# Attention with decay, a gated product and a SwiGLU layer on one core: a second set of Q and K tiles, movable copies, and a scheduler with other durations

## The chip, the core and the metric

The kernel runs on one core of a Trainium2 chip. Five engines work side by side: TensorE (PE; the loading of its weights is listed as PEld), VectorE (DVE), ScalarE (ACT), GpSimd (POOL), and SyncE (SP), which issues the DMAs. They wait for each other through semaphores. The metric is device time in microseconds (us), the median of several runs.

## The reference

Three computations, with independent inputs, all in float32. Cut to what matters:

```python
# attention: q, k, v [4, 8, 576, 64], f [4, 8, 576]
scores = matmul(q, k.T) / sqrt(64)
cum = cumsum(log(clip(f, 1e-4, 1)), axis=-1)
scores = where(causal, -1e9, scores + cum[..., :, None] - cum[..., None, :])
attn = exp(scores - max(scores)); attn /= sum(attn) + 1e-9
x = matmul(attn, v)                    # 4 batches x 8 heads
# product of two projections: x [2304, 512], d_ff 1024
y = ((x @ w1) * (x @ w2)) @ w3 @ w_out
# second layer: x [2304, 512], d_ff 1536
xn = x / sqrt(mean(x * x) + 1e-6) * rms_g
g = xn @ w_gate
out = (g / (1 + exp(-g)) * (xn @ w_val)) @ w_out
```

The kernel chains them: the attention's result (as 2304 tokens of 512) is the x of the product, and its y is the x of the second layer.

## The kernel before

**Numbers.** Each float32 operand of a matmul is held as two tiles, a high part and a low part (value minus high part). A product takes three matmuls (high by high, low by high, high by low). Making the two parts is work for ACT, DVE and POOL: `sub` (L230) is the subtraction that makes a low part and may go to DVE or POOL, `scaled` (L238) a copy with a factor.

**Weights.** They arrive in units of 1 MB in four raw buffers (`nrm`, `ul`, `x`, `x1`). `unit` (L481 to L505) recovers each unit's values in place, 1024 columns at a time: an ACT Prelu (L496), a DVE TENSOR_SCALAR (L497) and a DVE SCALAR_TENSOR_TENSOR (L498). Then ACT copies the high part (L504), and a `sub` (L230) makes the low part, in one piece of 1024 columns or four of 256. The matrix w3 @ w_out is formed first (`wc_group`, L557 to L561, high part `Wch` on ACT, low part `Wcl` on DVE), so that the product layer is one matmul less deep.

**Heads.** For each of 32 heads: `prep` (L345 to L356) makes the high and low parts of Q/8 and K. Q's first low part is a DVE instruction with three operands (L352). The tiles Q1, Q2, K1 and K2 exist once, so a head's parts can be written only when the matmuls of the head before have read them. The two rows that carry the cumulated decay are loaded by a DMA for each (L355, L356), from a copy in DRAM that the start writes. The raw q and k have two buffers. `attn_s` then does the scores: matmuls (L367, L368) into PSUM, the row maxima with the mask on DVE (`row_max`, L384, a custom instruction), the exponentials with row sums on ACT (`row_exp`, L391). Transposes follow (PE L428, high part `PTh` on ACT L431, low part `PTl` on DVE L432), the product with V (PE L451 and L457, ACT copies one half, L461, DVE adds, L462), and for each pair of heads the normalization (PE L473, DVE L477).

**Layers.** `x_split` (L578, L579) makes the parts of the attention's result, `ab_group` (L590 to L600) the two projections and their product `u` (ACT L596, DVE L598) with its parts `uh` (ACT L599) and `ul` (DVE L600), `y_group` (L613) the product with Wc, `norm` (L628) the rms norm, `gv` (L714) and `wout` (L745) the second layer.

**The start** (L782 to L818) clips f, takes the logarithm (ACT L791), the running sum (DVE scan L792), its high part (a DVE cast, L794), its low part, and the rows of head 0; then it writes all rows to DRAM.

**What sets the order.** Every instruction is an entry of a list scheduler, `Plan` (L70 to L192). An entry has one or several engines it may go to, each with a planned duration (`t_dve`, `t_act`, `t_pool`, L210 to L217), what it reads and writes, and perhaps a due time. `begins` turns due times into latest starts from the end backwards; `order` goes through the program in planned time, gives each engine the entry with the smallest due time plus WAIT times the time by which it would start later than the first possible one, and adds MARGIN or MARGIN2 to the lag of results that come after the planned time MT. Constants (L41 to L51) give due times of heads, groups and units. The result is a fixed order for each engine.

Of the kernel before, what the change touches and what calls it, by code (L numbers as in the profile page):

```python
# [22 lines left out]
P = 128  # L23
# [7 lines left out]
CH = S // 2  # L31
# [3 lines left out]
NRAW = 4  # L35
# [34 lines left out]
class Plan:  # L70
# [54 lines left out]
    def order(self):  # L125
# [10 lines left out]
        dma = 0  # L136
# [59 lines left out]
def body(ctx, tc, q, k, v, f, w12, w3, wo1, wgv, wo2, g, out):  # L196
# [35 lines left out]
    def scaled(n, o, a, by, r=(), w=()):  # L232

        def run(e):
            if e == "ACT":
                A.activation(o, a, AF.Copy, scale=by)
            else:
                on[e].tensor_scalar(out=o, in0=a, scalar1=by, scalar2=1.0, op0=ALU.mult, op1=ALU.mult)  # L238

        plan.op([t_act(n), t_dve(n, 0.52, True), t_pool(n, 0.83)], run, r, w)  # L240
# [49 lines left out]
    Wch = [m1.tile([P, DM], F32R, name=f"Wch{i}") for i in range(KF)]  # L290
    Wcl = [m1.tile([P, DM], F32R, name=f"Wcl{i}") for i in range(KF)]
# [38 lines left out]
    def make_qk_rows():  # L330
        for t in (Q2, K2):
            V.memset(f32(t)[D:P, :], 0.0)
# [12 lines left out]
    def prep(h, at):  # L345
        p = h % 2
        a, b_ = rq[p][0:D], rk[p]
        act(S, lambda: A.activation(Q1[0:D, :], a, AF.Copy, scale=0.125), [("rq", p)], ["Q1h"], at)
        act(S, lambda: A.copy(K1, b_), [("rk", p, 0), ("rk", p, 1)], ["K1"], at)
        scaled(S, Q2[0:D, :], a, 0.125, [("rq", p)], ["Q2"])  # L350
        low = dict(out=Q1[D:P, :], in0=a, scalar=0.125, in1=f32(Q1[0:D, :]), op0=ALU.mult, op1=ALU.subtract)
        dve(S + 100, lambda: V.scalar_tensor_tensor(**low), [("rq", p), "Q1h"], ["Q1l"], at, lock=True)  # L352
        sub(S, K2[0:D, :], b_[0:D], f32(K1[0:D, :]), [("rk", p, 0), "K1"], ["K2"])
        if h:
            dma(9200, lambda: SP.dma_start(out=f32(Q2[D:D + 4, :]), in_=cq_d[h]), ["cdq"], ["rowq"], at)  # L355
            dma(9200, lambda: SP.dma_start(out=f32(K2[D:D + 4, :]), in_=cn_d[h]), ["cdn"], ["rown"], at)  # L356
# [20 lines left out]
    def row_max(h, ap, i, key, at):  # L377
# [558 lines left out]
```

## Time and profile before

| | us |
|---|---|
| median of 3 runs | 1038.04 |
| the runs | 1037.55, 1038.04, 1038.85 |
| profiled execution | 1038.35 |
| its span in the trace | 1036.6 |
| around the span | 1.75 |
| PE busy in the span | 992.6 |
| DVE, ACT, POOL busy | 555.5, 466.1, 186.8 |

PE is busy for 96% of the span, and for 91% of it the chain of work that ended last runs through PE. DVE makes up 6%. The mean granted clock of TensorE is 0.99 of full speed. The difference of span and PE's busy time lies almost all in the first sixth of the span, where the attention of the first batch and the unpacking of the weights run side by side. The rest of the heads (three batches) is spread between the matmuls of the layers later on.

### The profile page before, as it was taken

The page shows a single profiled execution, that of the slowest core. Times are in us where ns is not written, and L with a number is a line of the kernel's source. Part 1 is how long each engine was busy: PE and PEld are TensorE (multiplying, and loading weights), DVE is VectorE, ACT ScalarE, POOL GpSimd, SP SyncE. Part 2 cuts the span into 40 slices and gives each one's busy share as a digit, 9 for nine tenths or more (in the row PEclk, how much of TensorE's full clock was granted, in tenths as well). Part 3 has the DMA queues.
Part 4 walks back from the last instruction along what each step waited for, and adds up shares of the span by engine and source line. Part 5 has one row for each costly group of instructions (what it writes and reads, how often), then busy time and mean ns, then how long its engine had stood idle before and what let it go on. Part 6 is the DMA issues. An engine that isn't in the chain of part 4 may idle for free.

```text
span 1036.6 us, 15402 instructions
## 1 busy us (share of the span) xinstructions
PE 992.6 (96%) x5928; PEld 886.8 (86%) x5928; DVE 555.5 (54%) x1104; ACT 466.1 (45%) x1004; POOL 186.8 (18%) x222
## 2 busy tenths in 40 slices
PE   1799979999999999999999999999999999999997
PEld 1578869999999999999999888878888888888896
DVE  6889999757668676776557445532122112211121
ACT  4778887656665665665445434421121112111111
POOL 3535433322523132240220300000000000000000
PEclk9999989999999999999999999999999999999999
DMA  8554533111212121200432324312001000100000
GB/s 271 184 189 134 181 116 120 49 36 51 71 37 61 48 60 39 59 15 1 170 120 105 136 109 162 104 59 84 1 1 41 1 1 0 41 1 1 17 25 21
DMA packets 28161, 75.71 MB, mean 73 GB/s; under 512 B 3644, under 2 KB 12348, under 8 KB 23160
## 3 DMA queue, kind: packets, MB, share of 16 engines
q1 hardware_dynamic: 28088, 74.73, 22.1%
q8 instruction: 46, 0.75, 0.3%
q14 instruction: 27, 0.22, 0.1%
HBM read 64.69 MB, written 10.03 MB: 72 GB/s over the span
## 4 chain that ended last, share of the span: by engine, by line
PE 91%; DVE 6%; DMA 1%; ACT 1%; issue 1%; POOL 0%; ACTq 0%; DVEq 0%; POOLq 0%
PE bank L714 29%; PE bank L590 19%; PE bank L613 10%; PE wide L745 8%; PE bank L745 6%; PE bank L428 5%; PE wide L451 4%; PE bank L557 3%; PE bank L368 1%; PE bank L367 1%; PE wide L473 1%; PE wide L367 1%; PE wide L368 1%; PE wide L457 1%; DMA rk<-in_k 1%
## 5 line engine op out<-in xcount | busy, mean ns | idle before, releaser
L721 DVE TENSOR_TENSOR s<-bank,s 128x512 f32<-128x512 f32 (+1 forms) x60 | 38.3, 638 | 281.3 <-PE bank L714 281.3
L714 PE MATMUL bank<-xnh,wgh 128*128 128x512 f32 (+1 forms) x480 | 177.6, 370 | 0.0
L714 PE MATMUL bank<-xnl,wgh 128*128 128x512 f32 (+1 forms) x480 | 177.6, 370 | 0.0
L714 PE MATMUL bank<-xnh,wgl 128*128 128x512 f32 (+1 forms) x480 | 177.2, 369 | 0.0
L720 ACT ACTIVATE s<-bank 128x512 f32<-128x512 f32 (+1 forms) x60 | 33.3, 555 | 189.4 <-PE bank L714 189.2
L714 PEld LDWEIGHTS bank<-xnh,wgh 128*128 128x128 f32 x480 | 90.2, 188 | 16.9
L714 PEld LDWEIGHTS bank<-xnl,wgh 128*128 128x128 f32 x480 | 90.3, 188 | 16.4
L714 PEld LDWEIGHTS bank<-xnh,wgl 128*128 128x128 f32 x480 | 90.2, 188 | 16.1
L431 ACT CAST PTh<-bank 128x320 fp32r<-128x320 f32 (+3 forms) x128 | 64.7, 506 | 86.5 <-PE bank L428 74.4
L722 ACT CAST zh<-s 128x512 fp32r<-128x512 f32 (+1 forms) x60 | 34.7, 578 | 129.7 <-DVE s L721 129.7
L432 DVE TENSOR_TENSOR PTl<-bank,PTh 128x320 fp32r<-128x320 f32 (+3 forms) x128 | 74.7, 588 | 22.2 <-ACT PTh L431 21.4
L613 PE MATMUL bank<-uh,Wch 128*128 128x288 f32 x256 | 77.2, 302 | 0.0
L613 PE MATMUL bank<-ul,Wch 128*128 128x288 f32 x256 | 75.5, 295 | 0.0
L613 PE MATMUL bank<-uh,Wcl 128*128 128x288 f32 x256 | 75.3, 294 | 0.0
L723 DVE TENSOR_TENSOR zl<-s,zh 128x512 fp32r<-128x512 f32 (+1 forms) x60 | 39.1, 652 | 30.4 <-ACT zh L722 30.0
L451 PE MATMUL wide<-PTh,V 128*128 128x512 f32 (+4 forms) x160 | 53.2, 338 | 0.6 <-DVE nmaxb L384 0.5
L451 PE MATMUL wide<-PTl,V 128*128 128x512 f32 (+4 forms) x160 | 49.6, 326 | 1.9 <-DVE PTl L432 1.9
L596 ACT COPY a<-bank 128x288 f32<-128x288 f32 x64 | 25.6, 400 | 52.7 <-PE bank L590 52.4
L745 PE MATMUL wide<-wo2h,zh 128*128 128x512 f32 x120 | 47.9, 399 | 0.7 <-ACT o L755 0.7
L613 PEld LDWEIGHTS bank<-uh,Wch 128*128 128x128 f32 x256 | 48.1, 188 | 0.4
L613 PEld LDWEIGHTS bank<-ul,Wch 128*128 128x128 f32 x256 | 48.2, 188 | 0.3
L598 DVE TENSOR_TENSOR u<-bank,a 128x288 f32<-128x288 f32 x64 | 29.1, 455 | 35.5 <-PE bank L590 30.5
(281 smaller groups left out, 2589.2 us busy)
## 6 DMA issues: line engine op xcount, KB each, us to landing
raw<-in_wgv SPq DMA_DIRECT2D x12, 1024.0 KB
rk<-in_k SPq DMA_DIRECT2D x64, 144.0 KB
raw<-in_wo SPq DMA_DIRECT2D x6, 1024.0 KB
nrm<-in_w SPq DMA_DIRECT2D x5, 1024.0 KB
rv<-in_v SPq DMA_DIRECT2D x32, 160.0 KB
rq<-in_q SPq DMA_DIRECT2D x32, 144.0 KB
yn_d<-nrm SPq DMA_DIRECT2D x8, 576.0 KB
raw<-yn_d SPq DMA_DIRECT2D x4, 1024.0 KB
```

What stands on the lines that cost most here:

```text
L428: T.transpose(o[:, c * P:(c + 1) * P], PB[p][i][:, kb * P:(kb + 1) * P], ident)
L431: act(n, lambda: A.copy(PTh[:, pt:pt + n], o[:, lo:lo + n]), [], [("PTh", pt), key], at, 55)
L432: dve(n, lambda: V.tensor_sub(PTl[:, pt:pt + n], o[:, lo:lo + n], f32(PTh[:, pt:pt + n])), [("PTh", pt)], [("PTl", pt), key], at)
L451: pe(w, lambda s_=s_, o=o, w=w, c=c, kb=kb, m=m, src=src: T.matmul(t[:, o:o + w], V2[p][:, kb, :], src[:, c:c + w], start=(s_ == 0 and m = ...
L590: T.matmul(o, a, x[:, kt, :], start=(kt == 0 and i == 0), stop=(kt == KD - 1 and i == 2))
L613: T.matmul(o, a[:, es], x[:, ft, :], start=(ft == 0 and i == 0), stop=(ft == KF - 1 and i == 2))
L714: T.matmul(t[m], a[:, m, kt, :], x[:, kt, 0:n], start=(kt == 0 and i == 0), stop=(kt == KD - 1 and i == 2))
L720: act(n, lambda: A.activation(s_()[:, 0:n], t[0], AF.Silu), [("bank", b_[0]), "right"], ["s"], at)
L721: dve(n, lambda: V.tensor_mul(s_()[:, 0:n], t[1], s_()[:, 0:n]), [("bank", b_[1])], ["s"], at)
L722: act(n, lambda: A.copy(zh()[:, 0:n], s_()[:, 0:n]), ["s"], [("zh", zp)], at)
L723: dve(n, lambda: V.tensor_sub(zl()[:, 0:n], s_()[:, 0:n], f32(zh()[:, 0:n])), ["s", ("zh", zp)], [("zl", zp)], at, lock=True)
L745: T.matmul(acc2[t], a[:, ts_], w, start=(fb == 0 and i == 0), stop=(fb == KF2 - 1 and i == 2))
```

## The change

- The tiles for Q and K become one tile `qk1` with four parts. A second tile `qk2` of the same size takes the place that `uh` has later, and serves the odd heads of the first batch (`qk_of`). The parts hold q, not q/8; the factor 1/8 moves into the row maxima (scale -0.125 in place of -1), and the cumulated decay is multiplied by 8 at the start.
- `scaled` becomes `copy`. High parts of Q, K, V and of the weight units go through it, so each may be put on ACT, DVE or POOL. Q's first low part becomes a `sub` (DVE or POOL).
- The start's cast of the running sum goes to ACT with the factor 8.
- Durations: exp over n columns as n + 225 columns (before n + 110), the copy of the half with 180 instead of 55 added, Prelu with 210 added, longer scores and longer reciprocals.
- The scheduler: once it has chosen an entry that starts late, it puts a shorter one ahead that ends at most SLIP = 800 ns behind that start. DMAs begin at 4500 ns. MARGIN and MARGIN2 are 600 and 300 ns, and other constants are new.
- `Wch` and `Wcl` are one tile each.

The core of the diff:

```diff
-S0, TE, T1 = 14000, 11400, 14300
-LT, LP = 8000, 10500
-WC0, WCP = 30000, 9400
-FD, FR = 14000, 1.48
-WAIT = 2.0
-COLD = 19378
-MT, MARGIN, MARGIN2 = 135119, 321, 133
+S0, TE, T1 = 0, 9000, 14300
+LT, LP = 5000, 13000
+WC0, WCP = 20000, 9400
+FD, FR = 14000, 1.35
+WAIT, SLIP = 2.0, 800
+DMA0, COLD = 4500, 26000
+MT, MARGIN, MARGIN2 = 135000, 600, 300
...
+                fits = [c for c in can if c[0] < t and c[0] + c[2] < t + SLIP]
+                if fits:
+                    t, i, ns, lock = min(fits, key=lambda c: (by[c[1]] + WAIT * (c[0] - first), c[1]))
...
-    def scaled(n, o, a, by, r=(), w=()):
+    def copy(n, o, a, r=(), w=(), by=1.0):
...
         plan.op([t_act(n), t_dve(n, 0.52, True), t_pool(n, 0.83)], run, r, w)
...
+    qk2 = get("qk2", m1, [P, 4, S], F32R, tag="uh", name="qk2")
+    def qk_of(h):
+        i = h % 2 if h < H else 0
+        t = (lambda: qk1, qk2)[i]
+        return *(lambda t=t, m=m: t()[:, m] for m in range(4)), i
...
-        act(S, lambda: A.activation(Q1[0:D, :], a, AF.Copy, scale=0.125), [("rq", p)], ["Q1h"], at)
-        act(S, lambda: A.copy(K1, b_), [("rk", p, 0), ("rk", p, 1)], ["K1"], at)
-        scaled(S, Q2[0:D, :], a, 0.125, [("rq", p)], ["Q2"])
-        low = dict(out=Q1[D:P, :], in0=a, scalar=0.125, in1=f32(Q1[0:D, :]), op0=ALU.mult, op1=ALU.subtract)
-        dve(S + 100, lambda: V.scalar_tensor_tensor(**low), [("rq", p), "Q1h"], ["Q1l"], at, lock=True)
+        Q1, Q2, K1, K2, s_ = qk_of(h)
+        copy(S, lambda: Q1()[0:D, :], a, [("rq", p), ("rows", s_)], [("Q1h", s_)])
+        copy(S, K1, b_, [("rk", p, 0), ("rk", p, 1), ("rows", s_)], [("K1", s_)])
+        copy(S, lambda: Q2()[0:D, :], a, [("rq", p), ("rows", s_)], [("Q2", s_)])
+        sub(S, lambda: Q1()[D:P, :], a, lambda: f32(Q1()[0:D, :]), [("rq", p), ("Q1h", s_)], [("Q1l", s_)])
...
-        dve(cols + 12, lambda: V.tensor_tensor_reduce(out=o, in0=ap, in1=m, scale=-1.0, scalar=-NEG, op0=ALU.add, op1=ALU.min, accum_out=nmax[p][:n, i:i + 1]),
+        dve(cols + 12, lambda: V.tensor_tensor_reduce(out=o, in0=ap, in1=m, scale=-0.125, scalar=-NEG, op0=ALU.add, op1=ALU.min, accum_out=nmax[p][:n, i:i + 1]),
...
-        act(cols + 110, lambda: A.activation(o, o, AF.Exp, bias=nmax[p][:n, i:i + 1], scale=-1.0, accum_out=rsum[pr][:n, p, i:i + 1]),
+        act(cols + 225, lambda: A.activation(o, o, AF.Exp, bias=nmax[p][:n, i:i + 1], scale=-1.0, accum_out=rsum[pr][:n, p, i:i + 1]),
...
-            act(n, lambda cs=cs: A.copy(h_l()[0][:, cs], f32(lo()[:, cs])), [key, kl] + r_out, wh, at)
+            copy(n, lambda cs=cs: h_l()[0][:, cs], lambda cs=cs: f32(lo()[:, cs]), [key, kl] + r_out, wh)
...
-        dve(300, lambda: V.tensor_copy(hi.bitcast(F32R), cum), ["cum"], ["cq0"], -100)
+        act(S, lambda: A.activation(hi.bitcast(F32R), cum, AF.Copy, scale=8.0), ["cum"], ["cq0"], -100)
...
-        dve(S, lambda: V.tensor_scalar_mul(cn[:, 1::2, :], cq[:, 0::2, :], -1.0), ["cq", "cn1"], ["cn"], -90)
+        copy(2 * S, cn[:, 1::2, :], cq[:, 0::2, :], ["cq", "cn1"], ["cn"], -1.0)
```

Three places where the order of instructions changes. First DVE, at a unit of w3 in the raw buffer `raw_x` (the third of the raw buffers) during the first heads. L498 ends the unpacking of the unit, `w3_257<-raw_x_198,w3_257` are its low parts; the first fence is before.

```order
L498 SCALAR_TENSOR_TENSOR raw_x_198<-raw_x_198 128x1024
L432 TENSOR_TENSOR PTl_115<-bank1_60,PTh_114 128x320
L432 TENSOR_TENSOR PTl_115<-bank2_61,PTh_114 128x384
L230 TENSOR_TENSOR w3_257<-raw_x_198,w3_257 128x256
L352 SCALAR_TENSOR_TENSOR Q1_98<-rq0_92,Q1_98 64x576
L230 TENSOR_TENSOR w3_257<-raw_x_198,w3_257 128x256
L462 TENSOR_TENSOR x0_141<-wide_58,rq0_92 64x576
L497 TENSOR_SCALAR x1_142<-x1_142 128x1024
```

In the changed kernel (L521 and L520 are the old L498 and L497, L242 is a `copy`, L233 a `sub`):

```order
L521 SCALAR_TENSOR_TENSOR raw_x_174<-raw_x_174 128x1024
L520 TENSOR_SCALAR x1_123<-x1_123 128x1024
L242 TENSOR_SCALAR w3_244<-raw_x_174 128x256 x2
L233 TENSOR_TENSOR qk1_98<-rq0_92,qk1_98 64x576
L233 TENSOR_TENSOR w3_244<-raw_x_174,w3_244 128x256 x3
L242 TENSOR_SCALAR w3_244<-raw_x_174 128x256
L233 TENSOR_TENSOR w3_244<-raw_x_174,w3_244 128x256
L485 TENSOR_TENSOR x0_122<-wide_58,rq0_92 64x576
```

Three copies of the unit's high part now stand on DVE, and four of its low parts in place of two; the transposes' low parts (L432) don't stand between them any more.

Second ACT, from the program's first instruction to the exp of head 0's widest block. `tmp` is the running sum's input, `nrm` a weight unit. Before:

```order
L791 ACT_TABLE_LOAD
L791 ACTIVATE tmp_147<-tmp_147 68x576
L348 ACTIVATE Q1_98<-rq0_92 64x576
L349 CAST K1_100<-rk0_94 128x576
L496 ACTIVATE nrm_82<-nrm_82 128x1024
L391 ACT_TABLE_LOAD
L391 ACTIVATE PB4a_108,rsuma_118<-PB4a_108,nmaxa_116 128x576
```

In the changed kernel (L805 the Ln, L808 the scaled high part of the running sum, L412 the exp):

```order
L240 ACT_TABLE_LOAD
L240 ACTIVATE qk1_98<-rq0_92 64x576
L805 ACT_TABLE_LOAD
L805 ACTIVATE tmp_128<-tmp_128 68x576
L240 ACTIVATE V20_99<-rv0_96 128x5x64
L808 ACTIVATE x0_122<-tmp_128 68x576
L240 ACTIVATE x1_123<-x0_122 32x2x576
L240 ACTIVATE qk2_195<-rk1_95 128x576
L519 ACTIVATE nrm_82<-nrm_82 128x1024
L827 ACT_TABLE_LOAD
L827 ACTIVATE rows_c_121<-rows_c_121 4x1
L412 ACTIVATE PB4a_105,rsuma_115<-PB4a_105,nmaxa_113 128x576
```

One more table is loaded, ahead of the Ln; the table for the exp is loaded ahead of a small exp (L827; before, L812 ran at 151.3 us); and the copies for the running sum and `x1` stand on ACT.

Third SP, the DMAs from the writing of the decay rows on. `cq_d` and `cn_d` are these rows in DRAM, `rq` and `rk` the raw q and k. Before:

```order
L815 DMA cq_d_71<-x0_141 32x2304
L816 DMA cn_d_72<-x1_142 32x2304
L338 DMA rk0_94<-in_k 64x576
L337 DMA rq0_92<-in_q 64x576
L343 DMA rv1_97<-in_v 128x320
L343 DMA rv0_96<-in_v 128x320
L355 DMA Q2_99<-cq_d_71 4x576
L356 DMA K2_101<-cn_d_72 4x576
```

In the changed kernel (L357 to L359 load q and k, L375 and L376 the rows):

```order
L831 DMA cq_d_71<-x0_122 32x2304
L832 DMA cn_d_72<-x1_123 32x2304
L359 DMA rk1_95<-in_k 64x576
L357 DMA rq1_93<-in_q 64x576
L358 DMA rk1_95<-in_k 64x576
L359 DMA rk0_94<-in_k 64x576
L357 DMA rq0_92<-in_q 64x576
L375 DMA qk2_195<-cq_d_71 4x576
L375 DMA qk1_98<-cq_d_71 4x576
L376 DMA qk2_195<-cn_d_72 4x576
L376 DMA qk1_98<-cn_d_72 4x576
```

The rows of head 1 (into `qk2`) and head 2 (into `qk1`) stand behind the second load of `rq0`, for head 4.

## Rows read from the trace of the kernel before

**Rows 1.** Windows by stage; us, PE, PEld, DVE, ACT, POOL busy (instructions), PEclk, DMA, GB/s.

```profile
16.50:31.00 14.50, 8.13 (x31) 6.92 (x31) 10.23 (x26) 9.84 (x22) 2.92 (x4) 1.00 0.71 206
31.00:60.00 29.00, 21.53 (x103) 16.89 (x103) 27.13 (x45) 23.52 (x46) 13.86 (x12) 0.88 0.66 225
60.00:130.00 70.00, 69.08 (x399) 58.65 (x398) 62.25 (x133) 58.03 (x140) 32.35 (x37) 1.00 0.48 157
130.00:150.00 20.00, 13.05 (x73) 10.91 (x74) 19.48 (x32) 17.30 (x32) 6.92 (x6) 0.83 0.40 133
150.00:600.00 450.00, 449.25 (x3324) 437.81 (x3323) 309.72 (x686) 257.12 (x611) 117.73 (x134) 1.00 0.22 70
600.00:1031.00 431.00, 430.32 (x2002) 355.15 (x2001) 115.54 (x169) 95.99 (x152) 4.90 (x2) 1.00 0.11 37
```

**Rows 2.** PE's waits: line waited for: us in total, times, longest.

```profile
PE wide L367 <- DVE Q L352: 14.9, 1, 14.9
...
PE bank L590 <- DVE Wcl L561: 4.4, 1, 4.4
```

**Rows 3.** Windows from the first row maximum to the first y group.

```profile
17.60:39.60 22.00, 12.73 (x59) 10.38 (x59) 17.48 (x39) 18.34 (x40) 6.89 (x8) 0.96 0.64 189
39.60:143.10 103.50, 91.65 (x514) 76.40 (x512) 94.45 (x188) 84.37 (x185) 49.15 (x49) 0.96 0.52 174
143.10:187.50 44.40, 43.08 (x299) 40.67 (x300) 42.12 (x82) 32.91 (x73) 10.79 (x10) 0.95 0.30 97
```

**Rows 4.** DVE's waits from 39.6 to 187.5 us.

```profile
DVE PTl L432 <- ACT PTh L431: 4.9, 15, 0.6
DVE x L462 <- ACT rq L461: 1.8, 3, 0.7
```

**Rows 5.** DVE's instructions by form, 39.6 to 187.5: busy us, mean ns | idle before.

```profile
L352 DVE SCALAR_TENSOR_TENSOR Q<-rq,Q 64x576 fp32r<-64x576 f32 x10 | 7.7, 775 | 0.3
...
L497 DVE TENSOR_SCALAR nrm<-nrm 128x1024 uint32<-128x1024 uint32 x5 | 3.4, 687 | 0.0
...
L497 DVE TENSOR_SCALAR raw_x<-raw_x 128x1024 uint32<-128x1024 uint32 x3 | 3.2, 1073 | 0.0
...
L230 DVE TENSOR_TENSOR w<-raw_x,w 128x256 fp32r<-128x256 f32 x4 | 2.7, 674 | 0.1
...
L230 DVE TENSOR_TENSOR K<-rk,K 64x576 fp32r<-64x576 f32 x3 | 2.2, 749 | 0.1
...
L238 DVE TENSOR_SCALAR rcol<-rinva 128x640 f32<-128x640 f32 x2 | 1.6, 820 | 0.1
...
L230 DVE TENSOR_TENSOR W1l<-raw_ul,W1h 128x1024 fp32r<-128x1024 f32 x1 | 1.2, 1221 | 0.0
...
L230 DVE TENSOR_TENSOR w<-raw_ul,w 128x256 fp32r<-128x256 f32 x2 | 1.1, 548 | 0.0
```

**Rows 6.** Timeline of the start: start us, us, engine, line, operation, [idle before <-releaser].

```profile
7.32 0.68 ACT L791 ACTIVATE tmp<-tmp 68x576 f32<-68x576 f32 x1 [5.30 <-DVE tmp L790]
...
8.18 1.36 DVE L792 TENSOR_TENSOR_SCAN tmp<-tmp 68x576 f32<-68x576 f32 x1
...
9.48 1.39 POOL L230 TENSOR_TENSOR K<-rk,K 64x576 fp32r<-64x576 f32 x1 [1.52 <-ACT K L349]
9.57 1.61 DVE L794 CAST x<-tmp 68x576 fp32r<-68x576 f32 x1
...
16.49 0.58 PE L368 MATMUL wide<-K,Q 128*128 128x288 f32 x1 [0.99 <-DVE K L810]
...
18.43 1.28 ACT L391 ACT_TABLE_LOAD   x1 [4.55 <-DVE nmaxa L384]
...
19.73 0.78 ACT L391 ACTIVATE PB4a<-PB4a,nmaxa 128x576 f32<-128x576 f32 x1
```

**Rows 7.** Timeline of PE: the first transposes, and the scores of head 1.

```profile
24.49 0.47 PE L428 MATMUL bank<-ident,PB1a 128*128 128x128 f32 x1 [4.97 <-ACT PB1a L391]
...
27.77 0.72 PE L367 MATMUL bank<-K,Q 128*128 128x448 f32 x1
```

More of the change, by code (lines that the diff above doesn't have):

```diff
@@ L328, in make_zeros, with get, fn, make_qk_rows @@
             G.memset(t, 1.0)
-    def make_qk_rows():
+    lazy = {}
+    def get(key, pool_, shape, dtype, **kw):
+        def fn():
+            if key not in lazy:
+                lazy[key] = pool_().tile(shape, dtype, **kw) if callable(pool_) else pool_.tile(shape, dtype, **kw)
+            return lazy[key]
+        return fn
+    Wch = get("Wch", m1, [P, KF, DM], F32R, name="Wch")
+    Wcl = get("Wcl", m1, [P, KF, DM], F32R, name="Wcl")
+    qk2 = get("qk2", m1, [P, 4, S], F32R, tag="uh", name="qk2")
[3 more added lines that the diff above has]
+        return *(lambda t=t, m=m: t()[:, m] for m in range(4)), i
+    def make_qk_rows(h, on=V):
+        _, Q2, _, K2, _ = qk_of(h)
         for t in (Q2, K2):
-            V.memset(f32(t)[D:P, :], 0.0)
+            on.memset(f32(t())[D:P, :], 0.0)
     def load_qk(h, at):
@@ L559, in wc_group @@
         at += step
-        act(512, lambda: A.copy(Wch[i], o), [], [("bank", n), ("Wch", i)], at)
-        dve(512, lambda: V.tensor_sub(Wcl[i], o, f32(Wch[i])), [("Wch", i)], [("bank", n), ("Wcl", i)], at)
+        act(512, lambda: A.copy(Wch()[:, i], o), [], [("bank", n), ("Wch", i)], at)
+        dve(512, lambda: V.tensor_sub(Wcl()[:, i], o, f32(Wch()[:, i])), [("Wch", i)], [("bank", n), ("Wcl", i)], at)
     clock = [0.0]
-    speed = [FR]
+    speed = [1.0]
     def tick(ns):
@@ L598, in ab_group @@
             dve(CH, lambda: V.tensor_mul(u, o, a), [("bank", n), ("a", fb % 2)], [("u", fb % 2)], at)
[L599 removed]
+            act(CH, lambda: A.copy(uh()[:, fb, :], u), [("u", fb % 2)], [("uh", fb)] + ([(x, 1) for x in QK] if b + c + fb == 0 else []), at)
             dve(CH, lambda: V.tensor_sub(ul()[:, fb, :], u, f32(uh()[:, fb, :])), [("u", fb % 2), ("uh", fb)], [("ul", fb)] + ([("raw", "ul")] if b + c == 0 else []), at, lock=True)
@@ L821, in body, with weights @@
     start()
+    def weights(units):
+        for kind, i, raw in units:
+            {"w3": w3_unit, "wo": wo_unit, "w12": w12_unit}[kind](i, raw, 0, 0)
     units = [("w3", 0)] + [("wo", i) for i in range(4)] + [("w3", i) for i in range(1, KF)] + [("w12", i) for i in range(KF)]
-    where = ["nrm", "ul", "x", "x1"][:NRAW]
+    where = ["nrm", "ul", "x", "x1"]
     for n, (kind, i) in enumerate(units):
@@ L827, in body @@
                 attention(h)
-        raw = where[n % NRAW] if n < 16 else "nrm" if i % 2 else "w3"
-        {"w3": w3_unit, "wo": wo_unit, "w12": w12_unit}[kind](i, raw, 0, 0)
+        weights([(kind, i, where[n % 4] if n < 16 else "nrm" if i % 2 else "w3")])
         if (kind, i) == ("wo", 3):
```

96 lines of the change are left out of this document (44 added, 52 removed).

## The prediction

> **What bounds the kernel now.** I read the stage windows first, for who is full and where. From 150 us to 1031 us PE is busy for 879.6 of 881 us, at full clock [rows 1]. The change leaves every matmul as it is (5922 in either order), so nothing that happens to VectorE or ScalarE behind 150 us can be worth more than the 1.4 us that PE is idle there. What can move is the stretch before: 16.5 to 150 us, in which PE is busy for 111.8 of 133.5 us.
>
> There the two rows to read are 31 to 60 and 130 to 150 us: DVE has 27.13 of 29 and 19.48 of 20 us, PE 21.53 and 13.05 [rows 1]. The list of PE's waits says the same: it stands 4.4 us in one piece for the last `Wcl` [rows 2]. Its 14.9 us for `Q` is the start, before the first matmul. So from the first row maximum to the hand-over DVE sets the pace. I therefore count what DVE has to do until the first `u`s for the first y group are made, since from there on PE has more work queued than it can do. DVE's idle time up to there is 22.00-17.48, 103.50-94.45 and 44.40-42.12, in sum 15.85 us [rows 3]. Of the 9.05 us in the middle stretch most are waits for ACT's results, `PTh` 4.9 and `rq` 1.8 us [rows 4].
>
> **The change part by part.** *Copies.* The hi copies of the weight units, of V and of Q and K may now go to DVE. Counted in the two orders from the first row maximum to the last `u` before the first y group, DVE gains 12 copies of 256 columns, 5 of 1024, 4 of 576 and one of 320: 10,816 columns. No such copy is in the trace of before on DVE. The nearest rows are the TENSOR_SCALARs over 1024 columns: 687 ns in one buffer, 1073 in another, beside POOL's work [rows 5]. By columns that is 7.3 us and 11.3 us. Small pieces cost more than their share, so I take 0.30, 0.75, 0.45 and 0.30 us: 3.6+3.75+1.8+0.3 = 9.45 us.
>
> *Subtractions.* Six more of 256 columns at 548 ns [rows 5] are 3.3 us (at 674 ns, 4.0), one more of V's 320 columns an estimated 0.6. One of 1024 columns goes to POOL (-1.2, from 1221 ns) and one `rcol` (-0.8) [rows 5]. Q1's low part is a subtraction instead of a three-operand instruction, twelve times 775 against 749 ns for K's [rows 5]: -0.3. With the copies DVE has 11.0 us more to do. ACT loses what DVE gets; ACT was busy for 84.37 of 103.50 us [rows 3] and is not the pace. This is the weak point of the change: work goes from the engine with room to the one without.
>
> *POOL.* To the same place POOL has 34 instead of 44 instructions with two inputs. One beside a DVE instruction costs it up to 1073-687 = 0.39 us [rows 5]; I take a third of that for each of the ten, since not all meet one: -1.3 us (0 to -3.9). At the start the same is seen: the cast of 576 columns takes 1.61 us at 9.57, while POOL subtracts from 9.48 to 10.87 [rows 6]. The Trainium skill, "SBUF — State Buffer", section "SBUF: two separate sides", calls the pair of ports that DVE and GpSimd share an exclusive lock, held for the whole instruction, while ScalarE has ports of its own. By that rule a copy moved from ACT to DVE also takes a place in that lock; the cast's row agrees, and the sum by the rule alone would lie nearer the 11.3 us for copies, so 1.9 us later.
>
> *Start.* Ln begins at 7.32, the scan of its result at 8.18 us [rows 6]. ACT now loads one table for a Copy and another for the Ln, a load of 1.28 us by the one in the trace [rows 6], and the scan moves from 8.18 to about 10. Against it the cast (1.61), Q1's low part and the scaling of `cn` leave DVE there. The first matmul with rows is at 16.49 [rows 6]; I put it 0.2 us earlier (between -2 and +1.5). The Exp's table is loaded by a dummy Exp, so its load is no longer between the row maximum and the first exp at 19.73 [rows 6]: the first exp comes 1.1 us earlier, and with it the first transposes, at 24.49 [rows 7].
>
> *Second set.* It lets head 1's Q and K be made while head 0 is used. But its S begins at 27.77 in before [rows 7], and in the new order the two loads of head 1's rows stand on SP behind the load of `rq0` for head 4, which waits for head 2's Q1 low part. SP issues nothing else while it stands. I estimate S of head 1 at 30.7, 3 us later. This costs nothing while DVE works on the raw units, which it does (27.13 of 29 us from 31 us on [rows 1]); without that cover it is +3 us at most. Later odd heads gain freedom, not a shorter chain.
>
> *Row maxima, wider slack.* The 1/8 is a constant in an instruction that runs anyway: nothing. MARGIN 600 and 300 in place of 321 and 133 act behind 135 us, where at most 1.4 us of PE's idle time are to be had: -0.5 to 0, I take 0. Wch and Wcl as one tile: 0.
>
> *Order.* Durations nearer to the trace (an exp over 576 columns is planned with 762 instead of 667 ns and measured with 0.78 us [rows 6]) and the gap filling should cut DVE's waits for ACT, and ACT is lighter by 21 copies of a weight unit's 256 columns. I take half of DVE's idle time away: 8 of 15.85 us stay. The bounds are 3 us, small latencies that no order removes, and all 15.85.
>
> *Sum.* +11.0 (DVE work) -7.85 (idle) -1.3 (POOL) -0.2 (start) = +1.65 us. The profiled execution took 1038.35 us, of which its span is 1036.6; it lies 0.3 above the median of 1038.04. So 1040.0 as profiled, and 1039.7 as the median.
>
> **The rivals.** *Faster, DVE's idle time goes.* If only 3 us of it stay and copies cost what the 687 ns row says with little more (7.8 us): 9.35-12.85-1.5 = -5.0 us, 1033; with 5 us left and copies at 8 us -2.8 us, 1035. For it: two thirds of the waits in the middle are for one engine that is relieved [rows 4], and the PE hole of 4.4 us is at a single place [rows 2]. Against it: they are 15 waits of at most 0.6 us [rows 4], the latency of a pair of engines that hand a bank over, and gap filling shortens such a wait only if another instruction fits.
>
> *Slower, DVE's idle time stays.* The place is 40 to 143 us. If DVE's waits for `PTh` and the half copy are hand-over latency, longer queues elsewhere don't remove them, and 11.0 us more work is 11.0-1.5 = +9.5 us: 1047.5. It decides against the time before as soon as more than 6.35+2.1 = 8.5 of the 15.85 us stay. For it: both waits are on results that PE has just finished, and ACT idles too in that stretch (19 us) [rows 3].
>
> *Slower, ACT's switches of tables cost more.* If ACT stands after each load for as long again, Ln and scan come later by another 1.4 us; with the 0.2 taken as gain gone it is +1.2, so 1040.9. In the trace the load from 18.43 lasts 1.28 and the exp starts at 19.73 [rows 6], 0.02 behind it, so nothing of the kind is seen. The Trainium skill, "ScalarE: Activation LUTs", section "What ACT_TABLE_LOAD costs", gives about 1283 ns for the load and about 1380 ns for a drain, for every switch. The load agrees with the row, the drain does not show behind it.
>
> *Slower, PE's clock.* The granted clock is 0.88 from 31 to 60 us and 0.83 from 130 to 150 us, the two stretches in which PE stands, and 1.00 with PE full [rows 1]: 0.17 of 20 us at half clock is 6.8 us. If the order spreads PE's holes into 60 to 130 us, and two more such pieces of 3.4 us come, PE loses 1.7 us in each: +3.4 on +1.65, 1042.8.
>
> That the second set does nothing is part of the forecast: nothing of the sum comes from it.
>
> **How the numbers follow.** A measurement of this kernel can tell about 0.2%, 2.1 us, from no change. The forecast (idle time 5 to 11 us left: -1.35 to +4.65, median 1036.7 to 1042.7) has 0.42: 0.02 faster, 0.28 same, 0.12 slower. The faster rival has 0.33, 1033 to 1035.9. Idle time that stays 0.11, 1043 to 1049. Tables 0.05, clock 0.09, both slower. So faster 0.35, same 0.28, slower 0.37. For 8 in 10 the range takes in the forecast, the faster rival, tables and clock, and the lower part of the idle time that stays: 1033 to 1047. Leaving out the ends, copies at 11.3 us and all idle time, costs 0.06 above; below, less than 3 us idle with copies at 7.3 us, 0.1.
>
> **What would show it.** The sum of DVE's busy time until the first y group should be 9 to 13 us higher, its idle time 5 to 11 us instead of 15.85, and a copy of 256 columns 0.22 to 0.40 us. S of head 1 should begin at about 30, the first exp below 19 us. The first y group's matmul should come within 2 or 3 us of before, and behind it PE be full as now. I am wrong if DVE's idle time falls below 4 us or stays above 12, if PE waits for ACT or POOL more than for DVE, or if PE shows a new hole behind 150 us.

## The result, and the profile after

The changed kernel takes 1028.28 us, the median of 4 runs (1027.78 to 1028.86), beside 1038.44 us (1037.55 to 1039.07) of the kernel before in the same comparison: a ratio of 0.9903, with a 95% interval from 0.9886 to 0.992. It is faster by 10.2 us. The prediction said 1039.7, in a range of 1033 to 1047. The span of the profiled execution is 1026.0 us in place of 1036.6.

The windows by stage of the changed kernel (us, PE, PEld, DVE, ACT, POOL busy, PEclk, DMA, GB/s) answer to [rows 1]:

```profile
16.50:31.00 14.50, 5.58 (x20) 4.38 (x20) 14.34 (x31) 7.57 (x19) 1.82 (x2) 1.00 0.55 145
31.00:60.00 29.00, 25.61 (x140) 20.95 (x140) 27.51 (x63) 25.01 (x55) 15.53 (x16) 1.00 0.76 258
60.00:130.00 70.00, 68.39 (x398) 57.63 (x397) 67.66 (x154) 56.65 (x130) 32.47 (x37) 1.00 0.52 163
130.00:150.00 20.00, 19.01 (x124) 16.62 (x122) 19.52 (x32) 12.14 (x28) 7.50 (x6) 1.00 0.39 131
150.00:600.00 450.00, 449.65 (x3292) 437.22 (x3291) 345.77 (x754) 238.49 (x573) 82.06 (x97) 1.00 0.23 75
```

Two rows carry the gain. From 31 to 60 us PE is busy for 25.61 instead of 21.53 us. From 130 to 150 us it is 19.01 instead of 13.05, and the granted clock is 1.00 instead of 0.83. So what looks like one loss in PE's row of before is two there: the time in which it stood, and the half clock, which the trace has from 140.4 to 147.2 us. From 16.5 to 31 us PE did less than before (5.58 for 8.13), and DVE, with 14.34 of 14.50 us, was full.

From 31 to 60 us the clock gave nothing back, although the row has 1.00 in place of 0.88. This trace has records of the clock from 37.4 us on (that of before from 31.2), and ahead of them a row shows 1.00. The matmuls tell more. Of these timelines of PE the first is the changed kernel's:

```profile
35.78 0.63 PE L474 MATMUL wide<-PTl,V 128*128 128x512 f32 x1
...
37.56 0.40 PE L571 MATMUL bank<-wo0h,w 128*128 128x512 f32 x1
```

```profile
55.83 0.63 PE L557 MATMUL bank<-wo3l,w 128*128 128x512 f32 x1
...
59.13 0.40 PE L557 MATMUL bank<-wo0h,w 128*128 128x512 f32 x1
```

A matmul over 512 columns takes 0.63 us at 35.78 us, as long as in the kernel before at 55.83, where the granted clock is 0.50, and 0.40 us once the clock is full. So the changed kernel ran at the lower of the two levels (1.2 and 2.4 GHz) until 37.4 us, about 6.4 us of this row, and the kernel before for 6.8 us of it (38.0 to 41.4 and 55.1 to 58.5).

The windows of the same kernel from its first row maximum to the first y group (176.3 us; 189.2 before), cut at the same places of the program as [rows 3]:

```profile
18.40:39.60 21.20, 12.40 (x53) 10.05 (x52) 20.43 (x47) 13.85 (x31) 6.74 (x5) 1.00 0.69 217
39.60:134.60 95.00, 90.24 (x524) 75.18 (x522) 91.84 (x203) 78.66 (x174) 45.28 (x51) 1.00 0.54 177
134.60:174.60 40.00, 38.86 (x274) 35.80 (x275) 39.40 (x73) 24.49 (x55) 10.22 (x9) 1.00 0.35 111
```

DVE's idle time is 0.77+3.16+0.60 = 4.53 us; it was 15.85. Its busy time is 151.67 us; it was 154.05. Neither number is what I wrote: I had 8 us of idle time and 9.7 us more work. In the list of DVE's waits of the changed kernel, 17 to 180 us, the largest is what had 4.9 us in [rows 4]:

```profile
DVE PTl L455 <- ACT PTh L454: 0.8, 2, 0.4
```

At the hand-over DVE makes the parts of x at 132.23 and PE's first projection begins at 133.34. Before, they began at 141.00 and 143.16, the latter with the wait of [rows 2]. In the changed kernel PE has no wait ahead of its first projection. The timelines of both engines in the changed kernel:

```profile
132.23 2.36 DVE L593 TENSOR_TENSOR xhl<-x,xhl 128x576 fp32r<-128x576 f32 x2
```

```profile
133.34 0.43 PE L604 MATMUL bank<-xhl,W0h 128*128 128x288 f32 x2
```

### The profile page after: what moved, and what is told of

It reads as the page before. It is cut to its first block, busy times and chain, and to the rows that moved or that the text cites. A ratio compares the mean times of both kernels' runs of the same rounds, so it can differ in the third digit from the quotient of the medians.

```text
span 1026.0 us, 15403 instructions
## 1 busy us (share of the span) xinstructions
PE 989.5 (96%) x5928; PEld 884.9 (86%) x5928; DVE 591.9 (58%) x1203; ACT 429.1 (42%) x944; POOL 148.3 (14%) x186
## 4 chain that ended last, share of the span: by engine, by line
PE 88%; DVE 8%; DMA 1%; issue 1%; ACT 1%; SPq 0%; DVEq 0%; ACTq 0%
PE bank L728 29%; PE bank L604 18%; PE bank L627 10%; PE wide L759 8%; PE bank L759 7%; PE bank L451 4%; PE wide L474 4%; PE bank L571 2%; PE bank L389 1%; PE bank L388 1%; DVE PTl L455 1%; DVE qk L233 1%; DMA raw_w<-in_w 1%; PE wide L388 1%; PE wide L389 1%
## 5 line engine op out<-in xcount | busy, mean ns | idle before, releaser
L455 DVE TENSOR_TENSOR PTl<-bank,PTh 128x320 fp32r<-128x320 f32 (+3 forms) x128 | 71.7, 583 | 16.2 <-ACT PTh L454 15.6
L454 ACT CAST PTh<-bank 128x384 fp32r<-128x384 f32 (+3 forms) x128 | 60.3, 505 | 29.6 <-PE bank L451 26.9
L474 PE MATMUL wide<-PTh,V 128*128 128x512 f32 (+4 forms) x160 | 49.9, 319 | 0.7 <-DVE nmaxb L405 0.5
L627 PEld LDWEIGHTS bank<-uh,Wcl 128*128 128x128 f32 x256 | 48.1, 188 | 0.0
L759 PE MATMUL wide<-wo2h,zl 128*128 128x512 f32 x120 | 47.5, 396 | 0.0
```

The costliest lines, as they stand in the source:

```text
L454: act(n, lambda: A.copy(PTh[:, pt:pt + n], o[:, lo:lo + n]), [], [("PTh", pt), key], at, 55)
L455: dve(n, lambda: V.tensor_sub(PTl[:, pt:pt + n], o[:, lo:lo + n], f32(PTh[:, pt:pt + n])), [("PTh", pt)], [("PTl", pt), key], at)
L474: pe(w, lambda s_=s_, o=o, w=w, c=c, kb=kb, m=m, src=src: T.matmul(t[:, o:o + w], V2[p][:, kb, :], src[:, c:c + w], start=(s_ == 0 and m = ...
L627: T.matmul(o, a[:, es], x[:, ft, :], start=(ft == 0 and i == 0), stop=(ft == KF - 1 and i == 2))
L759: T.matmul(acc2[t], a[:, ts_], w, start=(fb == 0 and i == 0), stop=(fb == KF2 - 1 and i == 2))
```

## The experiments

All changes of the order go through the scheduler, so every edit moves more than itself. For each kernel I give the median, the ratio to the kernel before of the same comparison with its interval, and two numbers of its trace: when DVE's first row maximum begins, and DVE's idle time from there to 1.7 us ahead of the first y group, the window of [rows 3]. Idle time is the window's length less DVE's busy time in it. Start, busy and idle time add up to the first y group by their definition, so the table tells where the time went, and not by itself that DVE sets the pace.

| kernel | us | ratio | first row maximum | DVE busy | DVE idle |
|---|---|---|---|---|---|
| before | 1038.4 | 1 | 17.6 | 154.05 | 15.85 |
| changed | 1028.28 | 0.9903 [0.9886, 0.992] | 18.4 | 151.67 | 4.53 |
| no_slip | 1045.23 | 1.0063 [1.0046, 1.008] | 20.0 | 152.64 | 13.26 |
| a_slip0 | 1037.84 | 0.9997 [0.9988, 1.0006] | 19.3 | 157.63 | 7.07 |
| unit_act | 1028.85 | 0.9906 [0.9891, 0.992] | 18.4 | 154.21 | 4.49 |
| one_set | 1031.52 | 0.9936 [0.9921, 0.9951] | 18.0 | 153.89 | 8.71 |
| a_old_dur | 1028.32 | 0.9901 [0.9886, 0.9916] | 17.6 | 150.89 | 6.41 |
| a_due | 1027.51 | 0.9893 [0.9879, 0.9908] | 18.6 | 154.46 | 3.74 |
| scatter | 1027.21 | 0.9889 [0.9874, 0.9903] | 17.8 | 153.11 | 3.19 |
| a_start | 1029.83 | 0.9916 [0.9902, 0.9931] | 20.6 | 152.25 | 4.45 |
| a_start_one | 1032.73 | 0.9942 [0.9927, 0.9957] | 18.4 | 158.68 | 2.72 |
| a_struct | 1025.56 | 0.9869 [0.9854, 0.9884] | 19.0 | 152.00 | 4.80 |
| b_slip | 1020.30 | 0.9824 [0.9809, 0.9838] | 15.8 | 149.90 | 4.60 |
| b_slip0 | 1035.82 | 0.9969 [0.9957, 0.998] | 17.0 | 153.40 | 12.60 |
| b_slip_dur | 1024.14 | 0.9865 [0.9848, 0.9881] | 16.3 | 151.30 | 5.40 |
| b_slip_copy | 1025.86 | 0.9876 [0.9861, 0.9891] | 16.3 | 154.51 | 3.69 |
| b_slip_due | 1022.84 | 0.9850 [0.9833, 0.9866] | 18.5 | 150.26 | 1.84 |
| b_slip_scatter | 1023.54 | 0.9852 [0.9836, 0.9869] | 16.5 | 150.63 | 4.37 |

After the result the theory was that the plan did it, gap filling and durations together (theory P). The rivals were the copies that may go to DVE (C), the second set (S), and a lucky order.

### One part of the change taken back

**unit_act**, the weight units' high copies on ACT alone.

```diff
-            copy(n, lambda cs=cs: h_l()[0][:, cs], lambda cs=cs: f32(lo()[:, cs]), [key, kl] + r_out, wh)
+            plan.op([t_act(n)], lambda e, cs=cs: A.copy(h_l()[0][:, cs], f32(lo()[:, cs])), [key, kl] + r_out, wh)
```

> The changed kernel, with the high copies of the weight units on ACT alone, as before; all else of the change stays. Theory P (the plan: gap filling and new durations took away DVE's idle time, the copies on DVE are load that this hides): DVE has fewer copies before the first y group, so the time stays or falls: 1025 to 1029 us, clock 1.00 from 31 us on. Rival C (the freedom to put copies on DVE took away the waits for ACT): DVE's idle time before the first y group goes back from 4.6 towards 15.85 us, and the time to 1034 to 1039.

The time is 1028.85, 0.6 us over the changed kernel, and DVE's idle time is unchanged. Rival C falls. Theory P has the time right, but two of its other statements are not borne out: the granted clock is 0.88 from 31 to 60 us, not 1.00, and DVE did not become lighter. Its window's row shows 154.21 us.

```profile
18.40:177.10 158.70, 140.49 (x855) 122.89 (x854) 154.21 (x317) 126.14 (x283) 56.02 (x58) 0.98 0.51 167
```

In the window DVE has 53 subtractions (L233) in place of 45, and POOL 26 in place of 34. What the copies leave free on DVE the scheduler fills with subtractions that POOL did.

**one_set**, one set of Q and K tiles. The clearing of the second set's rows stays in this program and falls on the first tile, so that the decay rows of one head are lost.

```diff
-        i = h % 2 if h < H else 0
+        i = 0
```

> The changed kernel with qk1 for every head, so that an odd head's Q and K wait again for the scores of the head before; the second tile is not used. Theory P: the second set is worth little, 1028 to 1031 us. Rival S (the second set lets the heads overlap, so DVE always finds something to do): PE waits for Q and K again, DVE idle 8 us or more before the first y group, 1033 to 1038 us.

1031.52 us, 3.2 more than the changed kernel, with DVE idle for 8.71 us. The idle time is what rival S named; the time lies between the two ranges, 0.5 us above theory P's and 1.5 below rival S's.

**no_slip**, without gap filling.

```diff
-                if fits:
+                if False:
```

> The changed kernel without gap filling: the chosen entry stands, no shorter one is put ahead of it. Theory P: DVE's waits for ACT's results come back, idle 10 us or more before the first y group, 1033 to 1038 us. Rivals C and S: 1028 to 1030 us, since copies and tiles are as free as in the changed kernel.

1045.23 us, 17 us more than the changed kernel and 0.6% above the kernel before. Without it the rest of the change, taken together, is a loss of 7 us. Theory P expected 1033 to 1038 us. The window's row, and the stage behind 150 us in the second fence:

```profile
20.00:185.90 165.90, 143.54 (x850) 122.01 (x848) 152.64 (x303) 114.97 (x255) 74.28 (x86) 0.99 0.46 153
```

```profile
150.00:600.00 450.00, 443.70 (x3280) 432.46 (x3279) 316.80 (x690) 221.75 (x567) 143.14 (x160) 1.00 0.20 65
```

DVE idles for 13.26 us again. And PE, which is busy for all but 0.35 us from 150 to 600 us in the changed kernel, stands for 6.3 us there, 3.4 of them behind the first y group (187.6 us): without gap filling the later heads wait too. I had no such loss in any of my rivals.

**scatter**, one due-time constant moved by 1%.

```diff
-S0, TE, T1 = 0, 9000, 14300
+S0, TE, T1 = 0, 9100, 14300
```

> The changed kernel with one due-time constant moved by 1% (TE 9100 for 9000), which means nothing for the work itself. It shows how far the time moves by another order alone. If the gain is in durations, copies and tiles: 1027 to 1030 us. If it is a lucky order: over 1033 us.

1027.21 us, 1.1 less. By this one neighbour the changed kernel is no lucky order.

**a_old_dur** and **a_due**, the old planned durations, and the old due times.

```diff
-        act(cols + 225, lambda: A.activation(o, o, AF.Exp, bias=nmax[p][:n, i:i + 1], scale=-1.0, accum_out=rsum[pr][:n, p, i:i + 1]),
+        act(cols + 110, lambda: A.activation(o, o, AF.Exp, bias=nmax[p][:n, i:i + 1], scale=-1.0, accum_out=rsum[pr][:n, p, i:i + 1]),
...
```

> The changed kernel with the old planned durations of exp, half copy, Prelu, scores and reciprocal; gap filling, tiles, copies, due times and margins stay. Theory G: 1028 to 1031 us. Rival D: DVE waits for ACT's results again, 1033 to 1040 us.

```diff
-S0, TE, T1 = 0, 9000, 14300
-LT, LP = 5000, 13000
+S0, TE, T1 = 14000, 11400, 14300
+LT, LP = 8000, 10500
...
```

> The changed kernel with the old due-time constants (S0, TE, LT, LP, WC0, FR and the starting speed); gap filling, durations, tiles, copies and margins stay. If the gain is gap filling's, DVE's idle time stays at 4 to 6 us and the time at 1028 to 1033. If the new due times make the early hand-over (first projections at 133 instead of 143 us), the hand-over is late again and the time 1035 to 1040.

1028.32 and 1027.51 us: neither the new durations nor the new due times earn anything by themselves in the changed kernel. Theory P is too wide; gap filling is what is left of it.

### Gap filling alone

**b_slip**, the kernel before with these three lines added, and **b_slip_dur**, with the new durations as well.

```diff
+                fits = [c for c in can if c[0] < t and c[0] + c[2] < t + 800]
+                if fits:
+                    t, i, ns, lock = min(fits, key=lambda c: (by[c[1]] + WAIT * (c[0] - first), c[1]))
```

> The kernel before with gap filling alone added to its scheduler (SLIP 800); tiles, copies, durations, due times and margins stay as before. Theory G (gap filling carries the gain by itself, since DVE's idle time is what it fills): DVE idle before the first y group falls from 15.8 to 5 to 8 us, 1029 to 1033 us. Rival F (gap filling needs the change's freer entries and durations, and alone only reshuffles): 1035 to 1042 us.

> The kernel before with gap filling and with the new planned durations (exp, half copy, Prelu, scores, reciprocal), nothing else. Theory G: like gap filling alone, 1028 to 1033 us, the durations worth 1 to 2 us. Rival D (the durations are what lets it fill the right gaps): this one 1028 to 1033 while gap filling alone stays above 1035. Rival F: both above 1035.

1020.30 us, 17.8 us below the kernel before and 8 us below the changed one: theory G, and more than it expected. With the durations it is 1024.14, 3.8 more, and rival D falls. The window's row of the first:

```profile
15.80:170.30 154.50, 144.40 (x867) 124.09 (x867) 149.90 (x321) 135.92 (x303) 54.72 (x52) 1.00 0.53 174
```

DVE's idle time is 4.60 us, as in the changed kernel; the start is 2.6 us earlier, the work 1.8 us less. This kernel beats both. Its first y group comes at 171.96 us, 17.2 earlier than before: 11.2 us by less idle time, 4.2 by less work and 1.8 by an earlier start. The rule acts on every engine, and no run limits it to DVE; that DVE's part carries the gain is argued from how full DVE is, not shown.

**b_slip0** and **a_slip0** put ahead only an entry that ends before the chosen one begins: SLIP 0 on the kernel before and on the changed one. The edit is shown against b_slip; in the changed kernel it is the constant SLIP.

```diff
-                fits = [c for c in can if c[0] < t and c[0] + c[2] < t + 800]
+                fits = [c for c in can if c[0] < t and c[0] + c[2] < t]
```

> The kernel before with gap filling where only an entry that ends before the chosen one begins is put ahead (SLIP 0 in place of 800). Theory I (it is idle time that is filled, and most gaps are shorter than an instruction, so without the slack hardly anything fits): DVE idle 10 us or more before the first y group, 1030 to 1037 us. Rival W (whole instructions fit, the slack adds little): 1020 to 1025.

> The changed kernel with SLIP 0. Theory I: between the changed kernel (1028) and the one without gap filling (1045), nearer to the latter: 1036 to 1044 us, DVE idle 9 us or more. Rival W: 1027 to 1032.

1035.82 and 1037.84 us. The gain without slack is 2.5 of 17.8 us on the kernel before, and on the changed one 7.4 of 17. Both times are as theory I expected, and so is the idle time of the first. It fits that most of DVE's waits are shorter than the instruction that would fill them ([rows 4]: 15 waits of at most 0.6 us): to fill them something due must be let begin up to 0.8 us late. In the second theory I missed DVE's idle time, "9 us or more". The windows' rows, first of the kernel before with SLIP 0, then of the changed one:

```profile
17.00:183.00 166.00, 148.36 (x870) 128.22 (x870) 153.40 (x317) 136.10 (x302) 48.99 (x52) 0.95 0.49 161
```

```profile
19.30:184.00 164.70, 146.69 (x849) 124.80 (x847) 157.63 (x326) 112.73 (x251) 61.12 (x67) 0.97 0.47 157
```

DVE idles for 12.60 and 7.07 us, and the clock is below 1.00 again. The second kernel pays in work, 157.63 us, 6.0 more than the changed kernel with slack, so idle time is not all that the slack takes away.

### What the rest of the change costs

**b_slip_scatter**, gap filling on the kernel before, with a due time moved by 1%.

```diff
-S0, TE, T1 = 14000, 11400, 14300
+S0, TE, T1 = 14000, 11510, 14300
```

> The kernel before with gap filling (SLIP 800) and one due-time constant moved by 1% (TE 11510 for 11400). If the 8 us to the changed kernel are in what the rest of the change does: 1019 to 1023 us. If they are the luck of one order: 1024 to 1030.

1023.54 us: 3.2 more for nothing, and between the two expectations. So about 3 us are what another order can make by itself, here and in the rows below, and nothing smaller is put down to an edit. The same 3 us may be luck in b_slip's own 1020.30, and in the 8 us to the changed kernel.

**b_slip_copy** and **b_slip_due** add to b_slip the movable copies of the weight units, and the new due times, margins, COLD and start of the DMAs.

```diff
...
+            plan.op([t_act(n), t_dve(n, 0.52, True), t_pool(n, 0.83)], run_copy, [key, kl] + r_out, wh)
```

> The kernel before with gap filling and with the high copies of the weight units on any of ACT, DVE and POOL. If these copies are part of what the changed kernel loses against the kernel before with gap filling (8 us): DVE's busy time before the first y group up by 3 us or more, 1023 to 1027 us. If they are free, as putting them back on ACT in the changed kernel showed (0.6 us): 1019 to 1021.5.

```diff
...
-MT, MARGIN, MARGIN2 = 135119, 321, 133
+MT, MARGIN, MARGIN2 = 135000, 600, 300
...
```

> The kernel before with gap filling and with the changed kernel's due times, margins, COLD and start of the DMAs; old tiles, copies and durations. If these constants cost part of the 8 us, 1023 to 1027 us, with later hand-over or PE waits in the first 60 us. If not, 1019 to 1022.

The copies make 1025.86 us, 5.6 more than b_slip but only 2.3 more than its neighbour b_slip_scatter. DVE's busy time is 4.6 us more than in b_slip (154.51 for 149.90), and nine of the copies stand on DVE, 4.2 us in all. That the copies cost here what they weigh, as I had argued for them, is likely, but one neighbour is too few to show it. The constants' 2.5 us lie within the scatter.

**a_start** puts the changed kernel's start back in the old order, **a_start_one** has one set of tiles as well, without the stray clearing.

```diff
-        copy(S, lambda: Q1()[0:D, :], a, [("rq", p), ("rows", s_)], [("Q1h", s_)])
+        copy(S, lambda: Q1()[0:D, :], a, [("rq", p), ("rows", s_)] + ["fc"] * (h == 0), [("Q1h", s_)])
-        act(S, lambda: A.activation(hi.bitcast(F32R), cum, AF.Copy, scale=8.0), ["cum"], ["cq0"], -100)
+        dve(300, lambda: V.tensor_scalar(out=hi.bitcast(F32R), in0=cum, scalar1=8.0, scalar2=1.0, op0=ALU.mult, op1=ALU.mult), ["cum"], ["cq0"], -100)
...
```

> The changed kernel with its start ordered as before: the logarithm comes before the first copy on ACT, so that no table is loaded between them; the high part of the running sum and the negated rows are made on DVE. Theory T (the changed start costs what it looks like against the kernel before with gap filling, whose first row maximum is at 15.8 us instead of 18.4): the first row maximum at 15.5 to 16.5 us, the time 1024 to 1027 us. Rival L (head 1's rows and the raw units are late anyway): the row maximum comes earlier, the time stays at 1027 to 1029.

> As the last one, and qk1 for every head; the clearing of the second set's rows is left out with it, so that every head is computed as in the reference. If the second set is worth 3 us, as the earlier run with one set says (its clearing of the second set's rows, left in, hit the first tile), 1027 to 1030 us. If that clearing made the 3 us, the same as with two sets, 1024 to 1027.

The first failed as an experiment: the first row maximum came at 20.6 instead of 18.4 us, later and not earlier, since other entries went ahead of it on DVE. 1029.83 us says nothing on what the changed start costs. The second, 1032.73, is 2.9 us above it. The second set is worth about 3 us in both pairs, with the same sign, but by idle time in one (8.71 for 4.53) and by work in the other (158.68 for 152.25), and 3 us is the scatter: likely, not shown.

**a_struct**, the changed kernel with old constants, old durations and the units' copies on ACT.

> The changed kernel with the old due times, margins, COLD, start of DMAs and planned durations, and with the weight units' high copies on ACT as before; left of the change are gap filling, the second set, unscaled Q and K with their copies and subtractions on any engine, and the new start. If tiles and start cost nothing, 1019 to 1023 us as the kernel before with gap filling. If they cost the 8 us, 1026 to 1030, with the first row maximum behind 18 us.

1025.56 us with a first row maximum at 19.0: between both expectations. Of the 8 us between b_slip and the changed kernel, 5.3 stay with tiles, copies of Q, K and V, and the start, less what the scatter makes (it lies 2.0 us above b_slip_scatter); how they divide among these is open. The start is the one that can be seen. The timeline of the changed kernel (start us, us, engine, line, operation, [idle before <-releaser]):

```profile
7.21 0.68 ACT L240 ACTIVATE qk<-rq 64x576 fp32r<-64x576 f32 x1 [5.20 <-DMA rq<-in_q]
...
7.91 1.28 ACT L805 ACT_TABLE_LOAD   x1
...
9.20 0.69 ACT L805 ACTIVATE tmp<-tmp 68x576 f32<-68x576 f32 x1
...
9.92 1.35 DVE L806 TENSOR_TENSOR_SCAN tmp<-tmp 68x576 f32<-68x576 f32 x1
```

and of b_slip:

```profile
6.25 0.68 ACT L794 ACTIVATE tmp<-tmp 68x576 f32<-68x576 f32 x1 [4.24 <-DVE tmp L793]
...
7.06 1.33 DVE L795 TENSOR_TENSOR_SCAN tmp<-tmp 68x576 f32<-68x576 f32 x1
```

In the changed kernel ACT takes a copy first, then loads the logarithm's table; the scan begins 2.9 us later, and the first row maximum 2.6 us later. The Ln begins 0.01 us behind the end of the load. The Trainium skill, "ScalarE: Activation LUTs", section "What ACT_TABLE_LOAD costs", has a drain of about 1380 ns for each switch to a different set; this trace doesn't show one, neither behind the load nor ahead of it, where the copy ends at 7.89 us and the load begins at 7.91.

## Why the prediction was wrong

**Where the time is decided: right.** In the changed kernel PE is full behind 150 us as before, and the time moves with the first y group: it comes 12.9 us earlier, 2.3 us more of the span lie behind it (849.7 for 847.4, since PE has done less by then), and the span fell by 10.6. In the stretch ahead of it DVE is busy for 151.67 of 156.20 us.

**Order: the step that failed first.** I let half of the idle time stay, "8 of 15.85 us", with 3 us as the least. 4.53 stayed. I took the waits for ACT for hand-over latency that gap filling could shorten "only if another instruction fits", and weighed that as a reason against. The SLIP of 0.8 us, which I had in the diff and described, means just that it need not fit: it may run up to 0.8 us over. a_slip0 is the changed kernel as I reasoned about it (7.07 us idle, 1037.84 us, inside my range), the changed kernel the one that was written (4.53, 1028.28); b_slip0 and b_slip show the same on the kernel before (12.60 and 4.60). For this term I was 3.5 us off.

**DVE's work: the larger miss.** I added 11.0 us and took 1.3 off for POOL; DVE's busy time fell by 2.4 us. But it had done less by the first y group, and about 4.5 us go with that: 12 heads' row maxima for 13, three fewer `PTl`, one fewer add of the half (L485). My sum had no such term. On the same footing DVE has some 2 us more to do, where I had 9.7. By kinds of instruction, counting each from its start or the end of the one before: the 22 copies are the ones that I had counted and make 10.6 us, where I had 9.45. The six more low parts of 256 columns make 0.1 us, where I had 3.3, since all 18 take 6.8 us and the 12 of before took 6.7. The rest is what else got cheaper. These are forms of the changed kernel, 17 to 180 us (busy us, mean ns | idle before), beside [rows 5]:

```profile
L521 DVE SCALAR_TENSOR_TENSOR nrm<-nrm 128x1024 uint32<-128x1024 uint32 x6 | 7.3, 1213 | 0.0
...
L520 DVE TENSOR_SCALAR raw_x<-raw_x 128x1024 uint32<-128x1024 uint32 x4 | 2.9, 723 | 0.0
...
L242 DVE TENSOR_SCALAR w<-raw_x 128x256 fp32r<-128x256 f32 x5 | 2.6, 531 | 0.3 <-PE bank L571 0.3
...
L233 DVE TENSOR_TENSOR w<-raw_x,w 128x256 fp32r<-128x256 f32 x6 | 2.4, 422 | 0.3
...
L242 DVE TENSOR_SCALAR w<-nrm 128x256 fp32r<-128x256 f32 x5 | 1.3, 290 | 0.3 <-PE bank L571 0.3
```

A low part of 256 columns takes 422 ns where I took 548 and had 674; the TENSOR_SCALAR on `raw_x` 723 for 1073 ns; on the unpacking of the units, 40 instructions in each kernel, the sum falls from 40.9 to 37.1 us. I gave POOL's relief 1.3 us (up to 3.9), and had read 1073-687 ns as the most that one meeting costs; both are means, and the three records behind the 1073 are 680, 1067 and 1471 ns. The trace says what stood beside the long instructions. Before, 11 of the 40 took clearly longer than the rest (a TENSOR_SCALAR more than 720, a SCALAR_TENSOR_TENSOR more than 1260 ns); in the changed kernel it is 4. Each of these 15 overlaps an instruction on POOL. But POOL's load by itself doesn't tell how many: its busy share of the window is about the same (66.83 of 169.9 and 62.25 of 156.2 us), and unit_act, where POOL has 26 instructions with two inputs in place of 34, has 8 long instructions. So POOL as the cause is argued from which instructions meet, not shown by a run.

The second part is that records of neighbours can overlap. The timeline of DVE in the changed kernel:

```profile
127.62 0.41 DVE L233 TENSOR_TENSOR w<-x,w 128x256 fp32r<-128x256 f32 x1
127.96 0.68 DVE L242 TENSOR_SCALAR W2h<-raw_x 128x1024 fp32r<-128x1024 f32 x1
128.56 1.01 DVE L455 TENSOR_TENSOR PTl<-bank,PTh 128x448 fp32r<-128x448 f32 x2
```

The first lasts to 128.03, the second begins at 127.96, and the third at 128.56 where the second lasts to 128.64. Where records overlap, an instruction costs 0.07 or 0.08 us less than its duration; behind a gap it costs all of it. So filling the gaps also made the old work cheaper: `PTl` is 48 instructions for 26.2 us before and 45 for 22.7 after, counted in this way, at nearly the same durations (mean 588 and 583 ns over the span).

The Trainium skill's rule on the shared port pair ("SBUF — State Buffer", section "SBUF: two separate sides"), an exclusive lock on the pair of ports that DVE and GpSimd share, is what I held against moving copies to DVE. That all the long unpacking instructions stood beside an instruction on POOL agrees with it. Its price for a moved copy no run isolates: b_slip_copy is slower by about what the copies weigh, and in the changed kernel unit_act shows no price.

**Start: wrong by 1 us.** The scan came at 9.92, as I had it (about 10). But the first matmul with rows came at 17.03 us, 0.5 us later instead of 0.2 earlier, and the first row maximum 0.8 us later. The four instructions that write head 0's rows (L823, L825) took 4.30 us in place of 2.89. Beside them, from 12.90 to 16.27 us, POOL cleared the second set's rows and made two copies of Q; before, POOL had one copy of 0.46 us there. What was freed on DVE behind them was taken by head 1's two subtractions (16.91 to 18.45 us). The exp came at 19.22 us, not before 19.

**Second set: right for head 1.** Its S begins at 28.06 us, without the rows, and then waits 2.53 us for them; the timeline of PE in the changed kernel:

```profile
31.31 0.71 PE L389 MATMUL bank<-qk 128*128 128x448 f32 x1 [2.53 <-DMA qk<-cn_d]
```

I had 30.7. It was covered later only: PE's busy time lies 1.5 us behind that of the kernel before at 30 us (6.18 for 7.71), and is level with it at 40 (14.77 for 14.82). Whether the later heads gain 3 us by the second set is what the runs left open.

**The clock: right row, wrong sign.** I named the half-clock stretches of [rows 1] only as something that could spread. The one from 130 to 150 us is gone with PE's hole there, and is back in b_slip0 (0.95 over its window); the 6.8 us from 31 to 60 us are made up by the lower level until 37.4 us. The rival's sum was also 0.3 us short: 1039.7 and 3.4 are 1043.1, not 1042.8.

**The faster rival** had the mechanism, with 3 to 5 us of idle time left, and a chance of 0.33. Its lower end, 1033, was too high, because the added work stood in it at nearly its full price. The range inherited this: its lower bound came from cheaper copies, and none came from the work that was there before getting cheaper.

## What to carry to other kernels

In a list scheduler, try a rule that lets a due entry begin a little late before tuning planned durations: here gap filling gave 17.8 and 17 us with 0.8 us of slack, and 2.5 and 7.4 with none, and the new durations gave nothing. Before pricing moved work by the durations of the old trace, ask whether these were measured beside another engine's instructions or behind gaps, and count what an instruction costs in a full row, from start to start. And where one edit changes the whole order, measure a neighbour of the same order first (1% of one constant made 1 and 3 us here), before a few microseconds are put down to an edit.

## What the runs showed of the hardware

Most of DVE's records overlap the one before by 0.06 to 0.09 us where an instruction follows at once (the three lines above; 263 of 307 in the changed kernel's window), so that the sum of durations is more than the time spent. Some never do: the add of the half (L485) and Q's low part (L233) always follow at 0.03 us. And the last step of the units' unpacking, the same instruction over the same 1024 columns, took 1.21 to 1.23 us in most cases, and up to 2.33 us before and 2.25 us in the changed kernel. The long instructions all overlap one on POOL, but some that overlap one are not long; which neighbour makes the difference wasn't measured alone. Last, a stage's row can print a clock of 1.00 where the trace has no record of it yet; matmuls of one size (0.63 and 0.40 us over 512 columns) tell the two levels apart.
